# A fused kernel's first batch: the engines' order up to the first gate product written by hand, one normaliser chain, and a tile for every raw weight

## The chip, the cores and the metric

The kernel runs on one core of a Trainium2 chip. The core has TensorE (PE) for matrix products, VectorE (DVE), ScalarE (ACT) and GpSimd (POOL) for work on elements, and DMA queues; the ones used here are issued from SyncE (SP) and from ScalarE. The metric is the device time of one execution in microseconds (us), as the median of several runs.

## What is computed

Three layers follow each other, for batches of 576 rows:

```python
kv  = einsum('bhsd,bhde', k, v)                       # linear attention, 8 heads of 64
out = einsum('bhsd,bhde->bhse', q, kv)
x   = out / sqrt(mean(out**2, -1) + 1e-6) * g_norm    # the normaliser
xk, xr = (mu * x + (1 - mu) * x_prev for mu in (mu_k, mu_r))   # x_prev: the row before
x2  = sigmoid(xr @ w_r) * (maximum(xk @ w_k, 0)**2 @ w_v)      # gate, keys, values
# then four experts of causal attention on x2, two per row by a gate
```

The inputs are float32, the weights w_r, w_k, w_v float64.

## The kernel before

There are eight batches of 576 x 512. Phase a does the linear attention, the gate and the keys, phase v the values, phase 2 the experts. The change is in phase a alone.

**Products.** Every float32 operand of a large product is split into a high and a low word (`split`), and a product is three of those (`mm3`): high by high, high by low, low by high. One group is 128 columns of weight by half a batch (288 rows), 12 products; a batch has 8 gate groups (`r_group`) and 16 key groups (`k_group`). They share four PSUM accumulators named `acc`.

**Weights.** w_r (4 pieces) and w_k (8 pieces of 128 x 512) come as 64-bit words, into tiles named `raw` or, for four of them, into the space of batch 1's `xT`; so at most four pieces can be under way. `converted` makes the two words of a piece: Abs on ScalarE, five steps on VectorE, copies on ScalarE, and three products with the identity on TensorE that correct the low word (L225 to L227). w_v is converted later, in `value_blocks`, which also builds the sums that phase v needs.

**The front of a batch** (`front`): k by v in five chunks (L293), the state copied to `kv` (L297), the queries by the state in four groups into `po` (L314), each evacuated by a Square and a copy (L318, L319), the means of the squares on TensorE (L332), the normaliser `rsqrt` on VectorE (14 steps, L338 to L353, result `rb`), spread back by TensorE (L361), and the scaling of `xT` (L364). For batch 0 this is done in two halves of 288 rows, each with its own chain. `mix` then makes the operands `mixh` and `mixl` from x and the row before: one ScalarE product (L416), one VectorE sum (L417), a copy (L418) and a subtraction (L410). For the gate of batch 0 the subtraction is done by TensorE and ScalarE instead (L406 to L408).

**Order.** The program is written as interleaved generators: `wconv` takes the next piece of weight, `wstep` one step of it between steps of the normaliser. What is written is not the final order. A scheduler simulates the program and orders each engine's instructions by its own times and priorities, and so draws forward what is ready. SP's queue loads k, v and q, then the small vectors; ScalarE issues the raw weights.

Of the kernel before, what the change touches and what calls it, by code (L numbers as in the profile page):

```python
# [25 lines left out]
def tile_kernel(ctx: ExitStack, tc: tile.TileContext, qT, k, v, g2, mu_k, mu_r, w_r, w_k, w_v, w_qk, w_vg, w_o, out):  # L26
# [31 lines left out]

    def split(hi, lo, src):
        nc.scalar.activation(hi, src, AF.Copy)  # L60
        nc.vector.tensor_sub(lo, src, hi.bitcast(F32))  # L61

    def mm3(ps, wh, wl, xh, xl, n):
        for i in range(n):
            nc.tensor.matmul(ps, wh(i), xh(i), start=(i == 0), stop=False)  # L65
            nc.tensor.matmul(ps, wh(i), xl(i), start=False, stop=False)  # L66
            nc.tensor.matmul(ps, wl(i), xh(i), start=False, stop=(i == n - 1))  # L67
# [102 lines left out]
    def phase_a():  # L170
        W["vb"] = ExitStack()
        vb = W["vb"].enter_context(tc.tile_pool(name="vb", bufs=1, side="right", reuse_waits="tile"))
        for name in BLOCKS:
            blk[name] = [vb.tile([P, KH, HM], F32R, name=f"w{u}_{name}") for u in "hl"]
        with ExitStack():
# [15 lines left out]
            first = []  # L191
            for b in range(2):
                first.append(sb.tile([P, NP, S + 1], F32, name="xT", bufs=2))
            spare = first[1].rearrange("p k t -> p (k t)")
            stg_ = ExitStack()
            stg = stg_.enter_context(tc.tile_pool(name="stg", bufs=1, side="right", reuse_waits="tile"))

            def low_word(lo, hi, ti, out, scale):
                nc.vector.tensor_scalar(hi, ti, -0x800000, None, op0=ALU.bitwise_and)
                yield  # L200
                nc.vector.scalar_tensor_tensor(out, lo.bitcast(U32), scale, hi.bitcast(F32), op0=ALU.mult, op1=ALU.mult)
                yield

            def high_word(hi, t):
                ti = t.bitcast(I32)
                nc.scalar.activation(t, hi.bitcast(F32), AF.Abs)
                yield
                nc.vector.tensor_scalar(t, t, TINY64, None, op0=ALU.max)
                yield
                nc.vector.tensor_scalar(ti, ti, 3, 0x3FFFFFF8, op0=ALU.logical_shift_left, op1=ALU.bitwise_and)  # L210
                yield
                nc.vector.scalar_tensor_tensor(ti, hi, -0x40000000, ti, op0=ALU.bitwise_and, op1=ALU.bitwise_or)
                yield
# [4 lines left out]
            def converted(raw, t, h, l):  # L218

                lo, hi = raw[:, :, 0], raw[:, :, 1]  # L220
                yield from high_word(hi, t)
                nc.scalar.activation(h, t, AF.Copy)
                yield from low_word(lo, hi, t.bitcast(I32), l, -2.0 ** -52)
                acc = acc_tile()
                nc.tensor.matmul(acc, ident, t, start=True, stop=False)  # L225
                nc.tensor.matmul(acc, idn, h, start=False, stop=False)
                nc.tensor.matmul(acc, idn, l, start=False, stop=True)  # L227
                nc.scalar.activation(l, acc, AF.Copy)

            wts = []  # L230
            raws = {}

            def wload(i):
                if i < len(wts):
                    _, _, w, r0, c0 = wts[i]
                    if i in (2, 3, 6, 7):
                        flat = spare[:, i % 2 * 2 * CW:(i % 2 + 1) * 2 * CW].bitcast(I32)
                    else:
                        flat = stg.tile([P, 2 * CW], I32, name="raw", bufs=2)
                    raws[i] = flat.rearrange("p (n t) -> p n t", t=2)  # L240
                    nc.scalar.dma_start(flat, w[r0:r0 + P, c0:c0 + CW].bitcast(I32))

            wat, cur = [0], []

            def wstep():
                if cur:
                    next(cur[0], None)

            def wconv():
                i = wat[0]  # L250
                wat[0] += 1
                if cur:
                    for _ in cur.pop():
                        pass
                if i < len(wts):
                    h, l, *_ = wts[i]
                    cur.append(converted(raws[i], fr.tile([P, CW], F32, name="cvt", bufs=3), h, l))
                    wstep()
                if 0 < i < 7 or 8 < i < 11:
                    wload(i + (3 if i < 7 else 1))  # L260
# [3 lines left out]
            def load_kv(i):  # L264
                b, c = divmod(i, NF)
                if b < B and i not in kvt:
                    t0, n = FH[c]
                    kt, vt = [fr.tile([P, DM], F32, name=name, bufs=5) for name in ("kt", "vt")]
                    nc.sync.dma_start(kt[:n], k[b, t0:t0 + n, :])
                    nc.sync.dma_start(vt[:n], v[b, t0:t0 + n, :])  # L270
                    kvt[i] = (kt, vt)

            def load_q(i):
                b, c = divmod(i, 4)
                if b < B and i not in qts:
                    qt = fr.tile([P, 2, HS], F32, name="qt", bufs=4)
                    nc.sync.dma_start(qt, qT[b, c])
# [4 lines left out]
            def front(b):  # L282
                kvp = acc_tile()
                kv = fr.tile([P, NP, D], F32, name="kv", bufs=1)
                kw = kvp[:, :NP * D].rearrange("p (a e) -> p a e", a=NP)
                for c, (t0, n) in enumerate(FH):
                    kt, vt = kvt[b * NF + c]
                    for a in range(NP):

                        for r in range(2):  # L290
                            hd = 2 * (2 * (a // 2) + r) + a % 2
                            hd = slice(hd * D, (hd + 1) * D)
                            nc.tensor.matmul(kw[r * D:(r + 1) * D, a, :], kt[:n, hd], vt[:n, hd],  # L293
                                             start=(c == 0 and a == 0), stop=(c == NF - 1), skip_group_check=True)
                    if b > 0 or c < 3:
                        load_kv((b + 1) * NF + c)
                nc.scalar.activation(kv, kw, AF.Copy)  # L297
                yield
                yield
                xT = xTs[b] = first[b] if b < 2 else sb.tile([P, NP, S + 1], F32, name="xT", bufs=2)  # L300
                nc.gpsimd.memset(xT[:, :, 0:1], 0.0)
                sqs = {}

                def cols(h):
                    return slice(1 + h * HS, 1 + (h + 1) * HS)

                def heads(h, a):
                    i = 4 * b + 2 * h + a
                    qt = qts[i]
                    po = pf.tile([P, 2, 512], F32, name="po", bufs=2)  # L310
                    for c in range(2):
                        for r in range(2):
                            rs = slice(r * D, (r + 1) * D)
                            nc.tensor.matmul(po[c * D:(c + 1) * D, r, :HS], kv[rs, 2 * a + c, :], qt[rs, c, :], start=True, stop=True, skip_group_check=True)  # L314
                    if b > 0:
                        load_q(i + 4)
                    sq = sqs[h, a] = fr.tile([P, 2, HS], F32, name="sq", bufs=4)
                    nc.scalar.activation(sq, po[:, :, :HS], AF.Square)  # L318
                    nc.scalar.activation(xT[:, 2 * a:2 * a + 2, cols(h)], po[:, :, :HS], AF.Copy)  # L319

                sm = []
                QS = HS // 2
                ms, y, nt, rb = [fr.tile([P, QS], F32 if name != "rb" else F32R, name=name) for name in ("ms", "y", "nt", "rb")]

                def means(*hs):
                    if not sm:
                        sm.append(acc_tile())
                    for i in range(NP):
                        for h in hs:
                            for c in range(2):  # L330
                                g = 32 * (2 * h + c)
                                nc.tensor.matmul(sm[0][g:g + 32, :QS], sels[:, i, :], sqs[h, i // 2][:, i % 2, c * QS:(c + 1) * QS],  # L332
                                                 start=(i == 0), stop=(i == NP - 1), skip_group_check=True)

                def rsqrt(h0, h1):
                    g = slice(64 * h0, 64 * h1)
                    m, r, t, c = ms[g], y[g], nt[g], rb[g]
                    nc.vector.tensor_scalar(m, sm[0][g, :QS], -0.5, -0.5e-6, op0=ALU.mult, op1=ALU.add)  # L338
                    wstep()
                    nc.vector.tensor_scalar(t.bitcast(I32), m.bitcast(I32), 1, None, op0=ALU.logical_shift_right)  # L340
                    wstep()
                    nc.vector.tensor_scalar(r.bitcast(I32), t.bitcast(I32), -1.0, float(0x5F3759DF + 2 ** 30 - 2 ** 22), op0=ALU.mult, op1=ALU.add)
                    wstep()
                    for _ in range(3):
                        nc.vector.tensor_mul(t, r, r)
                        wstep()
                        nc.vector.tensor_mul(t, t, m)
                        wstep()
                        nc.vector.scalar_tensor_tensor(r, t, 1.5, r, op0=ALU.add, op1=ALU.mult)
                        wstep()  # L350

                    nc.vector.tensor_copy(c, r)
# [726 lines left out]
```

## Time and profile before

| | us |
|---|---|
| median of 3 runs (lowest, highest) | 1014.84 (1014.62, 1015.19) |
| the profiled execution, its span | 1015.07, 1013.2 |
| busy: TensorE, VectorE, ScalarE, GpSimd | 966.5, 638.1, 540.6, 417.1 |

TensorE is busy 95% of the span. The page's 40 slices, about 25 us each, show that its idle time is nearly all in the first six and that its clock is below full there. A profile's busy TensorE isn't the same as TensorE at full speed: it may run at a lower granted clock.

### The profile page before, as it was taken

Reading aid. Unit: us, or ns where it says so; the run is one execution under the profiler, and the core shown is the slowest. Engines: PE = TensorE matmul, PEld = TensorE weight load, DVE = VectorE, ACT = ScalarE, POOL = GpSimd, SP = SyncE. Lnnn points to the kernel's source line nnn. Section 1 sums busy time; section 2 is a strip of 40 time slices with the busy share of each in tenths; the row PEclk is TensorE's granted clock in tenths of the full one; section 3 lists DMA queues with packets and bytes.
Section 4 is the critical chain, followed back from the end, with each engine's and each line's share of the span. In section 5 each row is a group of like instructions: output and inputs, shape, how many; then the busy total and the mean of one; then the engine's idle time right before and its main releaser. Section 6 shows DMA issues by size and latency. Waiting matters only on the chain.

```text
span 1013.2 us, 21245 instructions
## 1 busy us (share of the span) xinstructions
PE 966.5 (95%) x7960; PEld 877.9 (87%) x7960; DVE 638.1 (63%) x1538; ACT 540.6 (53%) x1334; POOL 417.1 (41%) x510
## 2 busy tenths in 40 slices
PE   5679989999999999999999999999999999999998
PEld 2359879998999999999899999888989888888986
DVE  4868978455463726359888885566575555656552
ACT  4666666555565655545444443356463645464544
POOL 0005545131222213276787777445161625334321
PEclk8889989999999999999999999999999999999999
DMA  9563362635446322676676652202020202020102
GB/s 349 160 197 124 120 222 91 209 107 185 159 134 191 105 80 77 197 251 200 212 241 202 209 165 94 71 22 60 37 79 17 94 2 95 22 73 27 48 13 82
DMA packets 82742, 127.22 MB, mean 126 GB/s; under 512 B 7632, under 2 KB 58320, under 8 KB 82640
## 3 DMA queue, kind: packets, MB, share of 16 engines
q1 hardware_dynamic: 63152, 97.68, 29.3%
q10 hardware_dynamic: 19488, 28.19, 8.7%
q8 instruction: 63, 1.03, 0.4%
q14 instruction: 39, 0.32, 0.1%
HBM read 78.66 MB, written 47.19 MB: 124 GB/s over the span
## 4 chain that ended last, share of the span: by engine, by line
PE 73%; DVE 8%; DMA 8%; ACT 5%; POOL 4%; issue 2%; SPq 0%; ACTq 0%; DVEq 0%; POOLq 0%
PE acc L65 15%; PE acc L66 15%; PE acc L67 14%; PE qa L629 6%; PE qd L629 4%; PE acc L629 4%; PE pt L898 3%; PE acc L925 3%; DMA x2in<-x2d 3%; PE s L849 3%; POOL x2l L735 2%; ACT pr L861 2%; DMA vraw<-in_w_v 2%; PE po L314 1%; POOL pr L878 1%
## 5 line engine op out<-in xcount | busy, mean ns | idle before, releaser
L447 POOL TENSOR_TENSOR ksq<-rl 128x288 f32<-128x288 f32 x128 | 96.8, 760 | 168.8 <-ACT rl L445 132.0
L66 PE MATMUL acc<-mixl,wkh 128*128 128x288 f32 x512 | 153.4, 300 | 0.0
L65 PE MATMUL acc<-mixh,wkh 128*128 128x288 f32 x512 | 151.8, 296 | 0.0
L67 PE MATMUL acc<-mixh,wkl 128*128 128x288 f32 x512 | 150.7, 294 | 0.0
L878 POOL TENSOR_SCALAR pr<-pr,rc,wg 128x512 f32<-128x512 f32 (+3 forms) x128 | 76.7, 613 | 100.3 <-DVE wg L808 53.2
L861 ACT ACTIVATE pr<-pr,nm 128x256 f32<-128x256 f32 (+4 forms) x144 | 83.2, 579 | 65.0 <-DVE nm L815 64.8
L410 DVE TENSOR_TENSOR mixl<-xm,mixh 128x288 fp32r<-128x288 f32 x120 | 57.4, 514 | 91.3 <-ACT mixh L418 83.9
L66 PEld LDWEIGHTS acc<-mixl,wkh 128*128 128x128 f32 x512 | 96.4, 188 | 1.6
L641 POOL TENSOR_TENSOR sgv<-ct,sgv 128x288 f32<-128x288 f32 x64 | 82.4, 1313 | 35.2 <-DVE ct L639 34.7
L67 PEld LDWEIGHTS acc<-mixh,wkl 128*128 128x128 f32 x512 | 96.6, 189 | 0.0
L445 ACT ACTIVATE rl<-acc 128x288 f32<-128x288 f32 x128 | 51.8, 405 | 83.7 <-PE acc L67 66.5
L65 PEld LDWEIGHTS acc<-mixh,wkh 128*128 128x128 f32 x512 | 96.3, 188 | 0.1
L65 PE MATMUL acc<-mixh,wrh 128*128 128x288 f32 x256 | 78.9, 309 | 0.4 <-ACT rl L445 0.4
L815 DVE CUSTOM_DVE_ANT_0 pr<-s,mask 128x256 f32<-128x256 f32 (+4 forms) x144 | 66.9, 482 | 18.6 <-PE pt L898 11.8
L66 PE MATMUL acc<-mixl,wrh 128*128 128x288 f32 x256 | 76.7, 300 | 0.2 <-ACT mixl L408 0.2
L67 PE MATMUL acc<-mixh,wrl 128*128 128x288 f32 x256 | 76.5, 299 | 0.0
L65 PE MATMUL acc<-x2h,wqh 128*128 128x320 f32 (+1 forms) x240 | 74.3, 310 | 0.0
L67 PE MATMUL acc<-x2h,wql 128*128 128x320 f32 (+1 forms) x240 | 71.1, 296 | 0.0
L66 PE MATMUL acc<-x2l,wqh 128*128 128x320 f32 (+1 forms) x240 | 70.9, 295 | 0.0
L61 DVE TENSOR_TENSOR kk<-tv,kk 128x1152 fp32r<-128x1152 f32 x32 | 59.0, 1861 | 8.8 <-ACT kk L60 8.8
L898 PE MATMUL pt<-ident,pr 128*128 128x128 f32 x400 | 62.7, 276 | 1.1 <-ACT pt L907 0.5
L418 ACT ACTIVATE mixh<-xm 128x288 fp32r<-128x288 f32 x128 | 52.3, 443 | 10.2 <-DVE xm L417 10.1
(209 smaller groups left out, 2778.6 us busy)
## 6 DMA issues: line engine op xcount, KB each, us to landing
kkd<-ksq SPq DMA_DIRECT2D x128, 144.0 KB, 1.8
kin<-kkd SPq DMA_DIRECT2D x32, 576.0 KB, 4.9
qt<-in_qT SPq DMA_DIRECT2D x32, 288.0 KB, 4.6
sgd<-sg ACTq DMA_DIRECT2D x64, 144.0 KB, 2.8
sgv<-sgd SPq DMA_DIRECT2D x16, 576.0 KB, 3.8
x2d<-sgv SPq DMA_DIRECT2D x16, 576.0 KB, 2.8
out<-ob SPq DMA_DIRECT2D x28, 288.0 KB, 2.1
kt<-in_k SPq DMA_DIRECT2D x24, 256.0 KB, 4.5
```

The lines of the kernel that those rows point to most:

```text
L61: nc.vector.tensor_sub(lo, src, hi.bitcast(F32))
L65: nc.tensor.matmul(ps, wh(i), xh(i), start=(i == 0), stop=False)
L66: nc.tensor.matmul(ps, wh(i), xl(i), start=False, stop=False)
L67: nc.tensor.matmul(ps, wl(i), xh(i), start=False, stop=(i == n - 1))
L410: nc.vector.tensor_sub(xl[:, p, :], xp, xh[:, p, :].bitcast(F32))
L447: nc.gpsimd.tensor_mul(sq, rl, rl)
L629: nc.tensor.matmul(q[:, :HS], a[:, i, ms_], c[:, i, :], start=(start and i == 0 and n == 0), stop=(stop and i == KH - 1 and n == 2), skip_ ...
L641: nc.gpsimd.tensor_mul(g, c, g)
L815: nc.vector.tensor_tensor_reduce(out=pr[:R, k0:k0 + kn], in0=s[:R, :kn], in1=mk, scale=1.0, scalar=lo, op0=ALU.add, op1=ALU.min, accum_out ...
L861: nc.scalar.activation(pr[:, :L], pr[:, :L], AF.Exp, bias=nm, scale=-1.0, accum_out=sms[b, p, j][:, e2:e2 + 1])
L878: nc.gpsimd.tensor_scalar(pr[:, :L], pr[:, :L], rc[:, r:r + 1], wg, op0=ALU.mult, op1=ALU.mult)
L898: nc.tensor.transpose(pt[:, (i - i0) * P:(i - i0 + 1) * P], pr[:, k1 - P:k1], ident)
```

## The change

- While a flag is on, `vec`, `act` and `ten` (wrappers of the three engines) mark each instruction to be kept in program order. The flag is on from the first weight conversion to the fourth gate group of batch 0. The steps of pieces 5 and 6 of the weights, written behind that point, are not marked, and the scheduler may place them among the marked ones.
- Batch 0's front is written out: four w_r pieces with the chunks of k by v, all four query groups, one means, one normaliser chain over 128 rows, then per half the spreading, scaling and mixing, then four gate groups.
- All twelve raw pieces have tiles of their own, in the space that the w_v blocks use later. All but two are loaded by SP, the small vectors first.
- The low half of batch 0's gate operand is a subtraction on VectorE like everywhere else; `older` issues the ScalarE product of the next quarter a step earlier.
- Batch 0's keys do four column groups for both halves first, then the other four; w_k's second half is converted between them. Batch 0's gates are stored through SP.
- In `value_blocks` the Abs and the load of each w_v piece are kept in program order; the order of the sums changes, and work starts four groups later.

```diff
+    class InOrder:
+        def __getattr__(self, name):
+            f = getattr(self.engine, name)
+            return (lambda *a, **k: tc.keep_in_program_order(f(*a, **k))) if self.on else f
...
+            def wload(i, eng):
+                _, _, w, r0, c0 = wts[i]
+                raw = vb.tile([P, CW, 2], I32, name="raw", tag="blk", bufs=2 * len(BLOCKS))
+                eng.dma_start(raw.rearrange("p n t -> p (n t)"), w[r0:r0 + P, c0:c0 + CW].bitcast(I32))
...
                 def low(p):
-                    if b == 0 and which == "r":
-                        acc = acc_tile()
-                        nc.tensor.matmul(acc[:, :HS], ident, xp, start=True, stop=False)
-                        nc.tensor.matmul(acc[:, :HS], idn, xh[:, p, :], start=False, stop=True)
-                        nc.scalar.activation(xl[:, p, :], acc[:, :HS], AF.Copy)
...
+                    vec.tensor_sub(xl[:, p, :], xs[p], xh[:, p, :].bitcast(F32))
...
+            for u, src in ((g_sb, g2), (muk, mu_k), (mur, mu_r)):
+                nc.sync.dma_start(u, src)
+            for i in range(KD):
+                wload(i, (act, nc.sync)[i % 2])
...
+            for i in range(KD, len(wts)):
+                wload(i, nc.sync)
...
-            TK = [1, 0, 1, 1, 0, 1, 1, 1, 1, 1, 1]
-            wconv()
-            for i in range(7):
-                run(f0)
-                ticks(TK[i])
...
+            for e in (vec, act, ten):
+                e.on = True
...
+            for h in range(2):
+                for a in range(2):
+                    f0.heads(h, a)
+            run(cs[4])
+            f0.means()
+            f0.rsqrt()
+            run(cs[4])
...
+                for _ in mix(0, h, "r"):
+                    pass
+            f1.start()
             for m in range(KD):
                 r_group(0, 0, m)
+            for e in (vec, act, ten):
+                e.on = False
...
+            WK = [(8,), (8, 9, 8, 8), (8, 9), (9, 10, 9), (9, 10), (10, 11, 10), (10, 11), (11, 11, 11)]
...
-            for b in range(B):
+            for b in range(1, B):
```

The order that results, at three places. VectorE, kernel before, from the means of the first half (`ms`) into its chain; `nt` and `y` are the chain's, `cvt` and `raw` pieces of w_k:

```order
L338 TENSOR_SCALAR ms_268<-acc_317 64x144
L212 SCALAR_TENSOR_TENSOR cvt_365<-raw_265,cvt_365 128x512
L340 TENSOR_SCALAR nt_270<-ms_268 64x144
L208 TENSOR_SCALAR cvt_387<-cvt_387 128x512
L199 TENSOR_SCALAR raw_265<-cvt_365 128x512
L342 TENSOR_SCALAR y_269<-nt_270 64x144
L210 TENSOR_SCALAR cvt_387<-cvt_387 128x512
L201 SCALAR_TENSOR_TENSOR wkl_134<-raw_265 128x512
L345 TENSOR_TENSOR nt_270<-y_269 64x144
L212 SCALAR_TENSOR_TENSOR cvt_387<-raw_293,cvt_387 128x512
L347 TENSOR_TENSOR nt_270<-nt_270,ms_268 64x144
L199 TENSOR_SCALAR raw_293<-cvt_387 128x512
```

The same place in the changed kernel, where all rows marked L67 are kept in order:

```order
L67 TENSOR_SCALAR y_374<-nt_375 128x144
L213 TENSOR_SCALAR cvt_531<-cvt_531 128x512
L67 TENSOR_TENSOR nt_375<-y_374 128x144
L215 TENSOR_SCALAR cvt_531<-cvt_531 128x512
L213 TENSOR_SCALAR cvt_558<-cvt_558 128x512
L67 TENSOR_TENSOR nt_375<-nt_375,ms_373 128x144
L217 SCALAR_TENSOR_TENSOR cvt_531<-raw_160,cvt_531 128x512
L215 TENSOR_SCALAR cvt_558<-cvt_558 128x512
L67 SCALAR_TENSOR_TENSOR y_374<-nt_375,y_374 128x144
L204 TENSOR_SCALAR raw_160<-cvt_531 128x512
L217 SCALAR_TENSOR_TENSOR cvt_558<-raw_162,cvt_558 128x512
L67 TENSOR_TENSOR nt_375<-y_374 128x144
```

The chain now spans 128 rows and stands once; steps of w_k pieces (here two at a time) still stand between its steps, ten in all where the first chain had sixteen.

ScalarE, kernel before, from the first sigmoid (`sg`) on; `vraw` is a piece of w_v, `kv_558` batch 1's state:

```order
L436 ACT_TABLE_LOAD
L436 ACTIVATE sg_541<-acc_542 128x288
L437 DMA sgd0_73<-sg_541 128x288
L222 ACTIVATE wkh_133<-cvt_676 128x512
L458 DMA vraw_1368<-in_w_v 128x1024
L297 ACTIVATE kv_558<-acc_557 128x256
L228 ACTIVATE wkl_134<-acc_632 128x512
L436 ACTIVATE sg_641<-acc_642 128x288
L437 DMA sgd0_73<-sg_641 128x288
L206 ACTIVATE cvt_1444<-vraw_1368 128x512
L416 ACTIVATE xm_622<-xT_128,nur_89 128x288
```

ScalarE, changed kernel, from the second half's operand copies (`mixh_443`) to the sigmoids of the first half's gate groups:

```order
L67 ACTIVATE mixh_443<-xm_447 128x288
L67 ACTIVATE xm_456<-xT_307,nur_89 128x288
L67 ACTIVATE mixh_443<-xm_451 128x288
L394 ACTIVATE xm_671<-xT_307,nuk_88 128x288
L67 ACTIVATE mixh_443<-xm_456 128x288
L67 ACT_TABLE_LOAD
L67 ACTIVATE sg_467<-acc_468 128x288
L67 ACTIVATE sg_483<-acc_484 128x288
L394 ACTIVATE xm_673<-xT_307,nuk_88 128x288
L67 ACTIVATE sg_499<-acc_500 128x288
```

The loads and the Abs of w_v are gone from here, and the first sigmoid now stands behind the last operand copy of the second half.

SP's queue, kernel before, from its eleventh row; ten loads of k (`kt`) and v (`vt`) stand ahead, `qt` are queries:

```order
L277 DMA qt_160<-in_qT 128x576
L277 DMA qt_162<-in_qT 128x576
L277 DMA qt_165<-in_qT 128x576
L277 DMA qt_167<-in_qT 128x576
L513 DMA g_sb_85<-in_g2 128x1
L514 DMA muk_86<-in_mu_k 128x4
L515 DMA mur_87<-in_mu_r 128x4
L269 DMA kt_207<-in_k 128x512
```

SP's queue, changed kernel, from its first row:

```order
L504 DMA g_sb_85<-in_g2 128x1
L504 DMA muk_86<-in_mu_k 128x4
L504 DMA mur_87<-in_mu_r 128x4
L228 DMA raw_124<-in_w_r 128x1024
L228 DMA raw_128<-in_w_r 128x1024
L262 DMA kt_130<-in_k 128x512
L263 DMA vt_131<-in_v 128x512
L262 DMA kt_134<-in_k 128x512
```

The three small loads moved ahead of everything, and two w_r pieces ahead of k and v; the eight w_k pieces follow the queries.

## Rows read from the trace of the kernel before

**Rows 1.** busy time by stage: us, PE, PEld, DVE, ACT, POOL (x instructions), clock, DMA

```profile
0.00:52.30 52.30, 31.75 (x200) 17.20 (x201) 33.10 (x85) 27.71 (x52) 1.99 (x17) 0.87 0.73 247
52.30:88.20 35.90, 30.66 (x274) 23.56 (x273) 26.50 (x57) 25.38 (x58) 7.01 (x6) 0.90 0.59 182
88.20:116.05 27.85, 27.61 (x211) 26.81 (x210) 24.53 (x55) 15.09 (x40) 17.01 (x20) 1.00 0.34 114
116.05:173.45 57.40, 51.45 (x450) 46.26 (x449) 48.27 (x96) 37.50 (x93) 27.54 (x32) 0.94 0.47 157
173.45:408.30 234.85, 234.85 (x2242) 220.25 (x2241) 117.73 (x270) 133.96 (x325) 57.58 (x84) 1.00 0.42 137
```

**Rows 2.** whom TensorE waited for: us in total, times, longest

```profile
PE po L361 <- DVE rb L353: 5.6, 3, 4.8
```

**Rows 3.** TensorE in order of time: start, us, line, out<-in, count

```profile
52.33 0.30 PE L65 MATMUL acc<-mixh,wrh 128*128 128x288 f32 x1
...
57.18 1.13 PE L225 MATMUL acc<-cvt,ident 128*128 128x512 f32 x2
...
58.60 0.29 PE L65 MATMUL acc<-mixh,wrh 128*128 128x288 f32 x1
...
84.05 0.93 PE L332 MATMUL acc<-sq,sels 128*32 128x144 f32 x20
...
88.20 0.29 PE L65 MATMUL acc<-mixh,wkh 128*128 128x288 f32 x1
...
89.80 0.29 PE L65 MATMUL acc<-mixh,wkh 128*128 128x288 f32 x1
...
101.13 0.67 PE L361 MATMUL po<-rb,selb 32*128 32x144 f32 x8 [0.24 <-DVE rb L353]
...
117.97 2.55 PE L293 MATMUL acc<-vt,kt 128*64 128x64 f32 x80
...
127.27 1.20 PE L314 MATMUL po<-qt,kv 64*64 64x288 f32 x16 [2.71 <-ACT kv L297]
```

**Rows 4.** the start on TensorE, ScalarE and in the chain of waits

```profile
17.41 1.15 PE L293 MATMUL acc<-vt,kt 112*64 112x64 f32 x32
...
19.97 0.63 ACT L222 ACTIVATE wrh<-cvt 128x512 fp32r<-128x512 f32 x1 [2.79 <-DVE nuk L517]
...
22.87 0.65 ACT L318 ACTIVATE sq<-po 128x576 f32<-128x576 f32 x1 [1.36 <-PE po L314]
...
23.95 0.66 ACT L318 ACTIVATE sq<-po 128x576 f32<-128x576 f32 x1
...
14.35 5.36 DMA muk<-in_mu_k
```

**Rows 5.** the normaliser on VectorE, first half of batch 0, then batch 2

```profile
28.14 0.30 DVE L338 TENSOR_SCALAR ms<-acc 64x144 f32<-64x144 f32 x1 [1.52 <-PE acc L332]
...
38.00 0.35 DVE L353 SCALAR_TENSOR_TENSOR rb<-rb,lom,y 64x144 fp32r<-64x144 f32 x1
...
191.34 0.31 DVE L338 TENSOR_SCALAR ms<-acc 128x144 f32<-128x144 f32 x1 [1.50 <-PE acc L332]
...
196.05 0.37 DVE L353 SCALAR_TENSOR_TENSOR rb<-rb,lom,y 128x144 fp32r<-128x144 f32 x1
```

**Rows 6.** the first low-half operand copy on ScalarE

```profile
41.74 0.43 ACT L418 ACTIVATE mixh<-xm 128x288 fp32r<-128x288 f32 x1
```

**Rows 7.** four microseconds after a pause of TensorE, columns as in rows 1

```profile
142.00:146.00 4.00, 4.00 (x22) 3.59 (x16) 2.41 (x7) 2.19 (x6) 0.95 (x2) 0.50 0.66 205
```

**Rows 8.** the DMA queue of SP from 420 to 440 us: packets, MB, share

```profile
q1 hardware_dynamic: 3966, 5.64, 83.6%
```

**Rows 9.** a w_v piece on ScalarE, TensorE behind it, its landing

```profile
65.82 0.66 ACT L206 ACTIVATE cvt<-vraw 128x512 f32<-128x512 f32 x1 [5.02 <-DMA vraw<-in_w_v]
...
67.51 1.33 PE L406 MATMUL acc<-xm,ident 128*128 128x288 f32 x2 [3.52 <-DVE xm L417]
...
58.36 7.43 DMA vraw<-in_w_v
```

More of the change, by code (lines that the diff above doesn't have):

```diff
@@ L243, in phase_a @@
[L243 to L260, printed above, removed]
+            wts, raws = [], []
@@ L321, in front @@
[L321 to L327, printed above, removed]
+                            ten.matmul(po[c * D:(c + 1) * D, r, :HS], self.kv[rs, 2 * a + c, :], qt[rs, c, :], start=True, stop=True, skip_group_check=True)
+                    load_q(i + 4)
+                    sq = self.sq[h, a] = fr.tile([P, 2, HS], F32, name="sq", bufs=4)
@@ L381, in front, with cols @@
+            QS = HS // 2
+            def cols(h):
+                return slice(1 + h * HS, 1 + (h + 1) * HS)
+            def front(b):
+                f = Front(b)
+                f.start()
+                for c in range(NF):
+                    f.chunk(c)
+                f.state()
+                yield
+                yield
                 for h in range(2):
                     for a in range(2):
-                        heads(h, a)
+                        f.heads(h, a)
                     yield
@@ new lines, in phase_a @@
+            f0, f1 = Front(0), Front(1)
+            run(cs[0])
+            f0.start()
+            for i in range(KD):
+                run(cs[i])
+                if i + 1 < KD:
+                    run(cs[i + 1])
+                run(cs[i])
+                run(cs[i])
+                if i == KD - 1:
+                    f0.chunk(NF - 1)
+                    f0.state()
+                run(cs[i])
+                if i < KD - 1:
+                    f0.chunk(i)
+                if i == KD - 2:
+                    f0.chunk(i + 1)
@@ new lines, in phase_a @@
+            mk = mix(0, 0, "k")
+            for m in range(KD + 1):
+                run(mk)
+                if m < 3:
+                    f1.chunk(m + 2)
+            f1.state()
+            mk = mix(0, 1, "k")
+            WK = [(8,), (8, 9, 8, 8), (8, 9), (9, 10, 9), (9, 10), (10, 11, 10), (10, 11), (11, 11, 11)]
+            mr = chain(mix(1, 0, "r"), mix(1, 1, "r"))
+            for n, (m0, h, m) in enumerate([(m0, h, m) for m0 in (0, KD) for h in range(2) for m in range(KD)]):
+                k_group(0, h, m0 + m)
+                if n < 4:
+                    f1.heads(*halves[n])
+                    run(mk)
+                if n == 3:
+                    run(mk)
+                for i in WK[n] if n < len(WK) else ():
+                    run(cs[i])
+                if n == 7:
+                    f1.means()
+                    f1.rsqrt()
+                if 8 <= n < 10:
+                    for a in range(2):
+                        f1.scaled(n - 8, a, f1.spread(n - 8, a))
+                if n > 10:
+                    run(mr, mr)
@@ L608, in phase_a @@
                         pass
-                    cvp[0].close()
             stk.close()
```

366 lines of the change are left out of this document (172 added, 194 removed).

## The prediction

> **What bounds the kernel now.** I read the table of busy time by stage first. I cut it at TensorE's first products of each stage: the first gate product at 52.3 us, the first key product of batch 0 at 88.2, the first product of batch 1 at 116.05, of batch 2 at 173.45, of batch 7 near 408. From 173.45 on TensorE is busy without a break at full clock: 234.85 us for five batches, 46.97 each [rows 1]. Nothing can be won there by order alone. Before that it is idle for 52.3 - 31.75 = 20.55, then 5.24, 0.24 and 5.95 us, 32.0 in all, and the granted clock is 0.87, 0.90 and 0.94 of full in three of the four stages. Batch 1 takes 57.40 where a later one takes 46.97, so 10.4 us are lost there alone. The table of waits then tells who is late: the largest single wait, 4.8 us, is for the normaliser `rb` [rows 2]. So the start and batches 0 and 1 are the whole question. On every engine the order after the w_v conversion, phases v and 2 included, is the same row for row, so what is won by 173 us should last to the end.
>
> **The change, part by part.** The work that TensorE must do is priced at full clock. One weight conversion (three products) goes from 57.18 to 58.60, 1.42 us; one group of twelve products from 88.20 to 89.80, 1.60; a batch's 80 k-by-v products 2.55; half of its query products 1.20; 20 of 32 passes of the means 0.93, so 1.5 a batch; half of the spreading 0.67, so 1.3 a batch [rows 3].
>
> *Start to the normaliser.* In the kernel before, the last k-by-v products ended at 17.41 + 1.15 = 18.56 us. The copy of the state came later, because on ScalarE it stood behind a weight copy that waited 2.79 us, by the profile for `nuk`, that is for the small load of mu_k that landed at 14.35 + 5.36 = 19.71 [rows 4]. The small loads now go first, so this wait goes. The added wait is that VectorE's first conversion steps now stand behind `nuk` and `nur`, and behind them ScalarE's copies and TensorE's checks of the first weight. The slowest landing seen, 5.36 us, would put them at about 7 us; this is inside the next bounds. The query products can begin no earlier than the w_r, k and v of batch 0 land (2.1 + 2.4 MB; 5.64 MB took 83.6% of 20 us on SP's queue alone, 337 GB/s while busy [rows 8], so 13.2 us after a start at about 2 us: 15), and on the rows of before no later than about 19. Three products of the last w_r piece now stand ahead of them. I take 18.0. Putting almost all loads on SP's queue I cost at nothing by the same row.
>
> All four query groups run now before the means, where two did before. Each costs ScalarE a Square and a copy, 23.95 - 22.87 = 1.08 us [rows 4]: 18.0 + 0.6 for the first products + 4.3, and the means end at about 23.0.
>
> *The normaliser.* One chain of 128 rows replaces two of 64. In the order its 14 steps have ten w_k conversion steps among them, since those are not pinned. Before, the first chain ran from 28.14 to 38.35, with 16 conversion steps: 30 steps in 10.2 us, 0.34 each. The bare chain of a later batch took 191.34 to 196.42, 5.1 us [rows 5]. These are the two ends; 24 steps at 0.34 give 8.2, and `rb` at 31.2.
>
> *To the first gate product.* Before, 38.35 to the first operand copy's end at 42.17 are 3.8 us [rows 6]. Four conversion steps now stand between, some 1.2 us beyond what lay there before. The first gate product comes at 31.2 + 5.0 = 36.2, against 52.33. The first group can't end before the fourth low half, about 3.3 us later: 39.5.
>
> *The gate stage.* From 39.5 TensorE has seven more groups (11.2), four conversions (5.7) and 2.55 of k by v: 19.4. Two waits come on top. TensorE restarts after a pause, and after such a pause it ran for four microseconds at 0.50 of its clock, 1.2 GHz [rows 7]; that costs 2.0. And the first sigmoid now stands on ScalarE behind the last operand copy of the second half (the second piece of the order), while one of the four accumulators is held for batch 1's state: the fourth group must wait for it, about 2.3. So the key products begin at 39.5 + 19.4 + 4.3 = 63.2 (before: 88.2, with batch 1's queries already done).
>
> The Trainium skill, "TensorE: Matmul & The Clock Gate", Part 1, says that the penalty of the clock's ramp is under 1% of a typical span and need not be fitted. By that the 2.0 would be dropped and the result would be 988. The rows put 0.50 into just these stretches, so I keep it.
>
> *The key stage of batch 0* now holds 16 groups (25.6), two halves of the queries (2.4), four conversions (5.7), the means and the spreading (2.8): 36.5, and batch 1 begins at 99.7 instead of 116.05: 16.4 us earlier. The second half of w_k is asked for only after eight groups, 13 us on; that hides its conversion.
>
> *Batch 1.* Before, its stage was crowded by all eight w_v pieces, which the scheduler had drawn forward, the first to 58 us [rows 9]. Now their Abs and their loads are pinned and lie in batches 1 to 6. I take the later batches' 46.97 plus 0.5 for a tight hand-over of the second half's operands: 9.9 gained. For the w_v steps spread over six dense batches I add 1.0; VectorE is busy there 117.73 of 234.85 us [rows 1], which is the cover.
>
> *Dropped and added steps.* The 16 low-half products of batch 0 and their eight copies on ScalarE go; eight subtractions on VectorE come, and they are inside the 3.3 above. The operand's older term is issued one step earlier in every mix; in the dense batches this is worth nothing.
>
> *Sum.* The profiled execution took 1015.07 (span 1013.2 and 1.9 around it), 0.2 above the median of 1014.84. 1015.07 - 16.4 - 9.9 + 1.0 = 989.8; I say 990.
>
> **Rivals.** *A: the w_v work hurts where it is put.* Its eight pieces with their adds on GpSimd now fall on batches that have no slack on TensorE. If each piece costs TensorE one 1.0 to 1.3 us stall, 8 to 10 us go: 998. For it speaks that the same pieces had a crowded batch 1 before; against it the half idle VectorE. The Trainium skill, "SBUF — State Buffer", Terms, says that VectorE and GpSimd lock a shared port pair against each other for a whole instruction; no row here separates that, and it would make this rival likelier.
>
> *B: ScalarE bounds the gate stage.* Between the first sigmoid and batch 1's state copy stand 35 of its instructions against 14.7 us of products on TensorE. At the 0.54 of a Square's slot (half of 1.08) they are 18.9, 4.2 more; with one more fall of the clock, 4 us, the result is 998.
>
> *C, the other side: a pinned Abs waits for its w_v piece.* Before, ScalarE once stood 5.02 us at such an Abs and TensorE 3.52 behind it, with a load that took 7.43 to land [rows 9]. With 2 us for the clock after such a pause, eight times 5.5 are 44: 1034, slower. In the order at least six groups, 9.6 us, lie between load and Abs, so it decides only where landings exceed that, and five of the eight must.
>
> *D: the change doesn't do what it says.* The pin orders only the pinned instructions, and the w_k steps among the chain grow to before's 16 and more, with late pieces to wait for; the gate products would start at about 45 and the result be 1000.
>
> *E: better.* The chain takes 5.1 to 6 and the accumulator wait is hidden: 984.
>
> **How the numbers follow.** The forecast, 984 to 996, 0.62; E below that 0.06; A 0.14; B 0.09; D 0.05; C 0.04. The range is 981 to 1003, which leaves out C, the far ends of A and B, and the best of E. Within 0.2% (2 us) is about what a measurement here can't tell from no change. All cases but C lie well below 1013: faster 0.93, same 0.02, slower 0.05, the last with a little for a start that goes wrong in a way not named.
>
> **What would show it.** The first gate product at 34 to 39 us; `rb` some 8 us after the means; a wait of TensorE before the fourth gate group; the first product of batch 1 at 97 to 103, and of batch 2 some 47.5 later. If batches 2 to 6 take over 47.5 each, A is right; idle TensorE between 45 and 63 with ScalarE full is B; an Abs of `vraw` that waits for its DMA is C. The forecast is wrong if batch 1 starts after 106, or if the gain by batch 2 is not still there at the end.

## The result, and the profile after

The changed kernel takes 998.30 us (median of 4 runs, 996.78 to 1002.44); the kernel before, run beside it, 1015.02 (4 runs, 1014.62 to 1016.80). The ratio is 0.9838, 95% interval 0.9806 to 0.9870. The gain is clear of the noise. The time lies inside the stated range of 981 to 1003, but outside the 984 to 996 of the forecast itself and 8 us above its 990. The profiled execution took 996.78, its span 995.0.

The busy table of the kernel after, TensorE alone (us, busy, instructions, clock, DMA share, GB/s), is cut at the first products of the same stages as [rows 1]: first gate product, first key product, batches 1 to 7.

```profile
0.00:38.05 38.05, 17.50 (x177) 0.88 0.97 333
38.05:62.62 24.57, 23.77 (x192) 0.90 0.30 102
62.62:100.18 37.56, 37.56 (x290) 1.00 0.44 136
100.18:150.35 50.17, 48.72 (x450) 1.00 0.51 161
150.35:201.16 50.81, 48.94 (x450) 0.97 0.50 160
201.16:248.45 47.29, 47.02 (x450) 1.00 0.50 167
248.45:295.42 46.97, 46.97 (x450) 1.00 0.52 169
295.42:342.60 47.18, 47.03 (x450) 1.00 0.52 166
342.60:389.93 47.33, 47.33 (x450) 1.00 0.23 79
389.93:995.00 605.07, 590.26 (x4594) 1.00 0.32 105
```

Batch 1 begins at 100.18 in place of 116.05, and batch 1 takes 50.17 in place of 57.40. But batches 2 to 6 take 239.58 together where before they took 234.85 [rows 1], and what follows lasts as long as before (605.07 against 1013.2 - 408.32 = 604.88). So 15.87 + 7.23 were won and 4.73 + 0.19 given back: 18.2, the difference of the spans.

The start, on VectorE and then TensorE (start, us, engine, line, out<-in, and in brackets the idle time before and who ended it; L67 is the helper through which all hand-ordered instructions pass):

```profile
25.13 0.31 DVE L67 TENSOR_SCALAR ms<-acc 128x144 f32<-128x144 f32 x1 [6.73 <-PE acc L67]
...
28.95 0.68 DVE L217 SCALAR_TENSOR_TENSOR cvt<-raw,cvt 128x512 int32<-128x512 int32 x1
...
33.16 0.37 DVE L67 SCALAR_TENSOR_TENSOR rb<-rb,lom,y 128x144 fp32r<-128x144 f32 x1
```

```profile
33.67 1.13 PE L67 MATMUL po<-rb,selb 32*128 32x144 f32 x8 [8.59 <-DVE rb L67]
...
38.05 0.61 PE L67 MATMUL acc<-mixh,wrh 128*128 128x288 f32 x1
...
47.78 0.40 PE L77 MATMUL acc<-mixh,wrh 128*128 128x288 f32 x1 [0.49 <-ACT sg L67]
```

`rb` is ready 8.4 us after the chain's first step (before: two chains, 28.14 to 38.35 for the first alone [rows 5]). The steps at L213 to L217 among them are w_k's. TensorE's wait for `rb`, 8.59 us, is the largest of the kernel after its first instruction, but it comes at 33.7 now.

Batch 1's loss. VectorE in the normaliser of batch 2's rows:

```profile
119.74 0.31 DVE L329 TENSOR_SCALAR ms<-acc 128x144 f32<-128x144 f32 x1 [0.83 <-PE acc L323]
121.77 0.43 DVE L213 TENSOR_SCALAR cvt<-cvt 128x512 f32<-128x512 f32 x1 [1.72 <-ACT cvt L211]
...
124.71 0.30 DVE L335 SCALAR_TENSOR_TENSOR y<-nt,y 128x144 f32<-128x144 f32 x1
125.05 1.35 DVE L333 TENSOR_TENSOR nt<-y 128x144 f32<-128x144 f32 x1
126.43 0.66 DVE L334 TENSOR_TENSOR nt<-nt,ms 128x144 f32<-128x144 f32 x1
...
130.92 0.37 DVE L338 SCALAR_TENSOR_TENSOR rb<-rb,lom,y 128x144 fp32r<-128x144 f32 x1
```

The chain takes 11.5 us where the bare one took 5.1 [rows 5]. A w_v piece stands between its steps, and the second instruction in the queue waits 1.72 us for that piece's Abs on ScalarE, with the chain behind it. Then steps that take 0.30 take 0.66 to 1.35. TensorE waits 1.45 us for this `rb`. The Abs itself comes late (121.08): ten microseconds before, ScalarE stood in front of the store of a gate tile, until a load of k had landed.

```profile
110.72 0.41 ACT L420 ACTIVATE sg<-acc 128x288 f32<-128x288 f32 x1 [2.16 <-DMA kt<-in_k]
```

Batch 2's loss. ScalarE (ACTq rows are DMAs that it issues), then TensorE:

```profile
156.81 0.34 ACTq L446 DMA_DIRECT2D vraw<-in_w_v  x1
...
162.79 0.33 ACTq L421 DMA_DIRECT2D sgd<-sg  x1
163.16 0.65 ACT L314 ACTIVATE sq<-po 128x576 f32<-128x576 f32 x1 [4.42 <-DMA vraw<-in_w_v]
```

```profile
164.41 0.71 PE L311 MATMUL po<-qt,kv 64*64 64x288 f32 x8 [1.87 <-ACT xT L315]
```

ScalarE stands for 4.42 us in front of the *store* of a gate tile, until the load of the next w_v piece has landed (issued at 156.81, landed 5.9 us later); the evacuation of the query products is queued behind it. TensorE stands 1.87 us, and this pause costs once more: from 166 to 169 the granted clock is 0.50, and its mean over 166 to 170 is 0.61.

```profile
162.00:166.00 4.00, 2.13 (x23) 0.96 1.06 312
166.00:170.00 4.00, 4.00 (x25) 0.61 0.91 287
170.00:174.00 4.00, 4.00 (x54) 1.00 0.26 86
```

Why should a store wait for a load? In the list of ScalarE's instructions both, in rows 193 and 197, name the same completion counter (a number that a DMA raises when it has landed):

```
193 L446 DMA vraw<-in_w_v 128x1024 [waits DMAHW6_49]
195 L421 DMA sgd_75<-sg 128x288 [waits DMAHW2_49,Activation_49]
197 L421 DMA sgd_75<-sg 128x288 [waits DMAHW6_49,Activation_49]
198 L314 ACTIVATE sq<-po 128x576 [waits PE_49]
```

The DMAs of SyncE and ScalarE take turns on eight counters, and a DMA waits until the one before it on its counter is done. The store of batch 1 shares its counter with the k load in the same way. That is theory 1; the rival is that the DMA engines are simply full there (share 1.06).

### The profile page after: what moved, and what is told of

The parts are those of the page before. It is cut to its first block, busy times and chain, and to the rows that moved or that the text cites. A ratio compares the mean times of both kernels' runs of the same rounds, so it can differ in the third digit from the quotient of the medians.

```text
span 995.0 us, 21152 instructions
## 1 busy us (share of the span) xinstructions
PE 955.1 (96%) x7936; PEld 871.4 (88%) x7936; DVE 643.1 (65%) x1532; ACT 538.8 (54%) x1326; POOL 414.4 (42%) x510
## 3 DMA queue, kind: packets, MB, share of 16 engines
q8 instruction: 63, 1.03, 0.4%
## 4 chain that ended last, share of the span: by engine, by line
PE 74%; DVE 8%; DMA 6%; ACT 6%; POOL 3%; issue 2%; SPq 0%; ACTq 0%; DVEq 0%; POOLq 0%
PE acc L77 15%; PE acc L78 14%; PE acc L79 14%; PE qa L671 6%; PE qd L671 4%; PE acc L671 4%; PE pt L940 3%; PE acc L967 3%; DMA x2in<-x2d 3%; PE s L891 3%; ACT pr L903 2%; POOL x2l L777 2%; PE acc L294 2%; POOL pr L920 1%; DMA vt<-in_v 1%
## 5 line engine op out<-in xcount | busy, mean ns | idle before, releaser
L397 DVE TENSOR_TENSOR mixl<-xm,mixh 128x288 fp32r<-128x288 f32 x120 | 59.8, 530 | 50.1 <-ACT mixh L403 49.6
L77 PE MATMUL acc<-mixh,wrh 128*128 128x288 f32 x240 | 73.9, 308 | 0.5 <-ACT sg L67 0.5
L79 PE MATMUL acc<-mixh,wrl 128*128 128x288 f32 x240 | 72.1, 300 | 0.0
L78 PE MATMUL acc<-mixl,wrh 128*128 128x288 f32 x240 | 72.0, 300 | 0.0
L72 ACT ACTIVATE kk<-tv 128x1152 fp32r<-128x1152 f32 x32 | 37.3, 1167 | 38.5 <-POOL tv L160 15.6
```

Source lines behind the costliest of these rows:

```text
L77: ten.matmul(ps, wh(i), xh(i), start=(i == 0), stop=False)
L78: ten.matmul(ps, wh(i), xl(i), start=False, stop=False)
L79: ten.matmul(ps, wl(i), xh(i), start=False, stop=(i == n - 1))
L397: vec.tensor_sub(xl[:, p, :], xs[p], xh[:, p, :].bitcast(F32))
```

## The experiments

All comparisons are with runs of the kernel before on the same chip. The table gives, from each profiled run, the start of the first gate product, of the first key product, of batches 1, 2, 3 and 7, the time from batch 7 to the end, and the median and ratio of the timed runs.

| kernel | gate | key | b1 | b2 | b3 | b7 | rest | median | ratio, interval |
|---|---|---|---|---|---|---|---|---|---|
| before | 52.33 | 88.20 | 116.05 | 173.45 | 220.43 | 408.32 | 604.9 | 1015 to 1017 | 1 |
| after | 38.05 | 62.62 | 100.18 | 150.35 | 201.16 | 389.93 | 605.1 | 998.30 | 0.9838 (0.9806-0.9870) |
| e2_store_sp | 38.12 | 62.69 | 100.24 | 148.78 | 196.11 | 384.32 | 607.8 | 994.22 | 0.9781 (0.9766-0.9795) |
| e1_load_sp | 39.17 | 63.73 | 101.28 | 153.14 | 201.72 | 395.57 | 605.7 | 997.35 | 0.9820 (0.9786-0.9854) |
| e3_later | 38.51 | 63.07 | 100.63 | 149.19 | 196.15 | 392.09 | 605.0 | 999.86 | 0.9825 (0.9787-0.9864) |
| e4_unpinned | 39.31 | 63.87 | 104.52 | 159.75 | 214.38 | 402.27 | 606.3 | 1010.19 | 0.9936 (0.9919-0.9952) |
| e5_pin_only | 52.34 | 84.08 | 111.60 | 160.47 | 208.50 | 404.35 | 605.2 | 1011.31 | 0.9956 (0.9932-0.9980) |
| e6_free_order | 38.03 | 62.39 | 99.95 | 150.24 | 204.24 | 393.67 | 610.2 | 1005.83 | 0.9885 (0.9864-0.9906) |
| e7_two_chains | 42.52 | 67.65 | 105.22 | 157.37 | 210.53 | 399.61 | 609.9 | 1011.04 | 0.9935 (0.9910-0.9960) |
| e8_best | 38.49 | 63.05 | 100.61 | 149.16 | 196.13 | 384.35 | 605.0 | 992.18 | 0.9758 (0.9735-0.9780) |
| e9_chain_clear | 34.15 | 59.50 | 97.48 | 146.03 | 193.01 | 381.22 | 609.1 | 992.11 | 0.9757 (0.9734-0.9780) |
| e11_kv_first | 44.02 | 69.18 | 106.73 | 155.28 | 202.26 | 390.47 | 608.0 | 1000.07 | 0.9837 (0.9815-0.9859) |
| e12_kv_clear | 40.68 | 64.13 | 102.42 | 150.97 | 197.95 | 386.70 | 607.3 | 994.61 | 0.9780 (0.9756-0.9804) |
| e13_tail_kept | 33.69 | 60.45 | 97.53 | 146.09 | 193.06 | 381.46 | 608.2 | 990.72 | 0.9741 (0.9723-0.9759) |

### Who holds ScalarE up in batch 2

**e2_store_sp**

```diff
-(nc.sync if b == 0 else act).dma_start(sgd[b][:, m, h * HS:(h + 1) * HS], sg)
+nc.sync.dma_start(sgd[b][:, m, h * HS:(h + 1) * HS], sg)
```

> Of the changed kernel, all stores of the gate (sgd) are issued by SyncE; ScalarE issues only the w_v loads. Theory 1: in batch 2 ScalarE stood 4.42 us because its store waits for the completion counter that the w_v load just issued also uses; with the stores on SyncE ScalarE has no such wait, batch 2 takes 47.0 to 48.0 us in place of 50.81, batch 1 keeps its slow normaliser chain (49.0 to 50.2), the whole is 993 to 996 us. Theory 2: the DMA engines, full at that time (share 1.0), are what delays, whoever issues: SyncE then holds its k and v loads back behind the stores, TensorE waits for kt or qt in their place, batch 2 stays at 50 to 51 and the whole at 997 to 1000.

```profile
100.24:148.78 48.54, 48.54 (x451) 1.00 0.53 166
148.78:196.11 47.33, 47.33 (x450) 1.00 0.54 171
156.00:162.00 6.00, 6.00 (x57) 1.00 1.03 330
```

Batches 1 and 2 lose their waits, with the DMA engines as busy as before (0.54, 171 GB/s). Where the stall had been, their share is 1.03 and the w_v load takes 7.7 us to land, yet TensorE is busy throughout. Theory 1 holds: full DMA engines go with a late landing, but alone they don't stop TensorE.

Batch 1 was expected to keep its slow chain (49.0 to 50.2) and takes 48.54:

```profile
119.94 0.30 DVE L329 TENSOR_SCALAR ms<-acc 128x144 f32<-128x144 f32 x1
...
128.59 0.77 DVE L338 SCALAR_TENSOR_TENSOR rb<-rb,lom,y 128x144 fp32r<-128x144 f32 x1
```

The w_v piece still stands among the steps and the chain still takes 9.4 us, but ScalarE no longer stands in front of a store in batch 1, the Abs comes at 118.86 in place of 121.08, and TensorE reaches `rb` at 129.75 without a wait. So the losses of both batches go with the stores.

One thing was not expected: the rest after batch 7 takes 2.7 us more. Of these, 1.6 are TensorE's own busy time: behind a wait of 1.77 us its clock is 0.63 from 456.3 to 460.3.

**e1_load_sp** (`act.dma_start` of the w_v load becomes `nc.sync.dma_start`)

> Of the changed kernel, the w_v loads are issued by SyncE, the stores of the gate stay on ScalarE. Theory 1 (shared counter): the w_v load falls on another counter in the list of waits; the stores of batch 2 then wait for k and v loads at most (landing 4.0 to 7.4 us after issue, issued earlier), ScalarE stands 0 to 2.5 us, batch 2 takes 47 to 49, the whole 994 to 997. Theory 2 (full DMA engines): the same bytes move in the same 10 us, ScalarE stands 3 us or more in front of a store, batch 2 50 to 51, the whole 997 to 1000.

The wait for `vraw` is gone from ScalarE. In its place stand waits of stores for k and v loads that precede them on their counters, in batches 1, 2, 4 and 5:

```profile
ACT sg L420 <- DMA vt<-in_v: 3.8, 2, 2.6
ACT sq L314 <- DMA kt<-in_k: 3.6, 1, 3.6
```

Batch 2 is 48.58 as expected, though ScalarE stands 3.6 us in it and not 2.5 at most; batch 1 is 51.86, batch 5 50.33. Moving the load only changes who is waited for, and the median, 997.35, lies between the two theories. (The profiled run is the slowest of its four, 1003.14; the others are 994.99 to 997.82.)

**e3_later** (`range(6)` becomes `range(14)` in `value_blocks`: the first w_v step comes eight groups later)

> Of the changed kernel, the first step of the w_v conversion comes 14 groups into batch 1 in place of 6, behind the normaliser chain of batch 2's rows. Theory A: the 11.5 us of that chain (119.7 to 131.3) come from the steps of the w_v piece that stand between its steps on VectorE; they are gone, the chain takes 5 to 6 us, TensorE's 1.45 us before the first spread are gone, batch 1 takes 48.0 to 49.0. Batch 2 has its w_v load elsewhere; it loses 0 to 4 us by whether a store shares its counter. The whole 993 to 998. Theory B: the chain is slow because of what GpSimd and ScalarE do there anyway (squares of the keys, Relu); it stays over 9 us and batch 1 over 49.8.

```profile
120.11 0.31 DVE L329 TENSOR_SCALAR ms<-acc 128x144 f32<-128x144 f32 x1 [0.87 <-PE acc L323]
...
124.08 0.70 DVE L337 CAST rb<-y 128x144 fp32r<-128x144 f32 x1
124.81 0.37 DVE L338 SCALAR_TENSOR_TENSOR rb<-rb,lom,y 128x144 fp32r<-128x144 f32 x1
```

Theory A holds for the chain: with the w_v piece elsewhere it takes 5.07 us in place of 11.5, TensorE no longer waits for it, and batch 1 takes 48.56. But no store holds ScalarE up in batch 1 here either, and e2 took TensorE's wait away with the piece left in the chain; so what the piece alone cost TensorE isn't shown. Batch 2 is clean too, 46.96; but now batch 4 takes 49.31 and batch 5 52.71, the latter by the same kind of wait, and the whole, 999.86, misses the 993 to 998 expected:

```profile
299.00 0.34 ACTq L446 DMA_DIRECT2D vraw<-in_w_v  x1
...
305.29 0.33 ACTq L421 DMA_DIRECT2D sgd<-sg  x1
305.66 0.65 ACT L314 ACTIVATE sq<-po 128x576 f32<-128x576 f32 x1 [4.71 <-DMA vraw<-in_w_v]
```

Here load and store share counter DMAHW4. The stall has moved with the turn of the counters.

### What the parts of the change are worth

**e4_unpinned** (`pinned = tc.keep_in_program_order` becomes `pinned = lambda i: i`) and **e5_pin_only** (the kernel before, with w_v's loads and Abs held in program order)

> Of the changed kernel, the w_v loads and the Abs that opens each piece are not held in program order. Theory A: the pin bought part of batch 1's 7.2 us; without it the scheduler puts the pieces of w_v early again, two or three of them beside the front of batch 2, batch 1 takes 53 to 57 us, later batches 47, the whole 1000 to 1005. Theory B: batch 1 gained because the conversions of w_k are elsewhere and buffers are free, not by the pin; batch 1 stays at 49.5 to 51, the whole within 2 us of 998.

> The kernel before, with one part of the change alone: its w_v loads and the Abs that opens each w_v piece are held in program order. Theory A: the pin is what takes the crowd out of batch 1 (without it, batch 1 of the changed kernel took 55.23 us and batch 2 54.63, with it 50.17 and 50.81); here batch 1 falls from 57.40 to 48 to 52, later batches stay within 3 us of 46.97 in sum, the whole 1007 to 1012. Theory B: in the kernel before, the w_v steps are hemmed in by the conversion of w_k and by the shared staging buffers, the pin alone moves nothing or makes a piece wait: batch 1 stays over 55, the whole 1013 to 1020.

In e4 batch 1 takes 55.23, batch 2 54.63: theory A, and its whole, 1010, is still above the 1000 to 1005 expected, since batch 0 also grew (65.21 against 62.13). In e5 batch 1 falls from 57.40 to 48.87, theory A again, and the gate stage from 35.87 to 31.74. But batches 2 to 6 give back 243.88 - 234.85 = 9.0 us, where 3 were allowed; ScalarE waits there for k, v and w_v loads, up to 4.8 us at once.

Against the kernel before, the pin alone gains 5.7 us, the rest of the change alone 6.2, both together 16.7. That is 4.8 more than their sum; whether each needs the other isn't shown, since waits elsewhere moved totals by as much in other runs (e6).

**e6_free_order** (`e.on = True` is never set)

> Of the changed kernel, nothing is held in program order up to the first gate group (the loads, tiles, one normaliser chain and the pins of w_v stay). Theory A: the order written by hand is what brings the first gate product from 52.33 to 38.05; without it the scheduler puts the conversion of w_k between the steps of the chain, and the first gate product comes at 42 to 50, the whole 1002 to 1010. Theory B: the loads in another order and the one chain do it; the first gate product comes at 37 to 40, the whole 996 to 1000.

Theory A is false as to the place. With the order left to the scheduler the first gate product comes at 38.03, as with the order written by hand (38.05); the chain begins 4.2 us later but has one w_k step between its own. Batch 1 begins at 99.95. The 7.5 us that it is slower come behind: batch 2 takes 54.00, 3.2 more, batch 5 48.11, the rest 610.2, 5.1 more.

```profile
ACT sq L314 <- DMA vraw<-in_w_v: 6.1, 1, 6.1
```

That is the store behind the w_v load once more, in batch 2. In the rest the scheduler's order is another one, and TensorE waits 3.7 us for an operand `vs` that cost it no wait before. So the hand-written order by itself bought nothing that this start shows, and a total can move by 7 us through places far from the edit.

**e7_two_chains**

```diff
-            f0.rsqrt()
+            f0.rsqrt(0, 1)
+            f0.rsqrt(1, 2)
```

> Of the changed kernel, batch 0's normaliser runs as two chains of 64 partitions, one behind the other, as in the kernel before (batch 1 on: one chain). Theory A: a step takes as long for 64 partitions as for 128, so 11 more steps of 0.31 to 0.36 us stand in front of the first scaled rows: the first gate product comes 3.5 to 5 us later, at 41.5 to 43, and as the gate stage runs back to back the whole is 3 to 5 us more. Theory B: steps on half the partitions are shorter or the first half's spread hides them; under 1.5 us more.

```profile
33.58 0.31 DVE L67 TENSOR_SCALAR ms<-acc 64x144 f32<-64x144 f32 x1
...
37.78 0.37 DVE L67 SCALAR_TENSOR_TENSOR rb<-rb,lom,y 64x144 fp32r<-64x144 f32 x1
```

A step takes 0.30 us on 64 partitions as on 128; the second chain adds 4.57 us, the first gate product comes 4.47 later, batch 1 5.04 later. That is theory A. The whole loses 12.7, more than the 3 to 5 expected: batches 1 and 2 take 52.15 and 53.16, the rest 609.9. The trace places most of it: ScalarE stands in front of the same two stores as in the changed kernel, now for 2.60 and 5.56 us, TensorE waits 1.46 and 2.96 behind them, and the clock of the two batches is 0.97 and 0.94; in the rest TensorE waits 3.8 for `vs`, as in e6. Why these waits are longer is open. Of the 14.28 us that the first gate product gained, the single chain is thus about 4.5; the remaining 9.8 are left to the loads and tiles by subtraction, not by a run of their own.

### Putting it together

**e8_best** (stores on SyncE except in the last batch, `range(14)`)

> Of the changed kernel, stores of the gate go to SyncE except in the last batch, and the first w_v step comes 14 groups into batch 1. Both theories by the runs so far: the stores keep ScalarE free of waits for loads (batch 2 47.0 to 47.4), the later start keeps the w_v steps out of batch 1's chain (48.5), the last batch's stores on ScalarE give back the 2.7 us that the tail lost with all stores on SyncE. Theory A, the three add up: batch 7 begins at 382.5 to 384.5, the whole 988.5 to 992. Theory B, they don't: a w_v piece falls into another batch's chain or the tail loses from another cause: 993 to 996.

```profile
100.61:149.16 48.55, 48.55 (x450) 1.00 0.51 164
149.16:196.13 46.97, 46.97 (x450) 1.00 0.52 169
...
384.35:989.30 604.95, 590.02 (x4594) 1.00 0.32 105
```

Theory A: batch 7 begins at 384.35 and the rest takes 604.95, which fits e2's loss there having come with the last batch's stores. That isn't shown: e9 to e13 leave these stores on ScalarE, and their rest takes 607 to 609. The median, 992.18, is 0.2 above the range and beats both kernels.

**e9_chain_clear** (e8, with the Abs of the w_k pieces pinned behind the first gate operands)

> The kernel of e8_best, with the conversion of w_k held behind the first rows of the gate mix, so that none of its steps stands in batch 0's normaliser chain. Theory A: the 8.57 us from the means to rb are 5.07 of the chain and 3.5 of w_k steps between; they go, and 0.9 of w_k steps between rb and the first gate product too: the first gate product comes at 33 to 35 in place of 38.5, the gate stage takes 24.6 to 26, the whole gains 2.5 to 5 us on e8_best. Theory B: VectorE is busy 20.2 of 24.5 us in the gate stage already and the 8 us of w_k steps come back there: the gate stage grows by 3 to 5 us and the whole stays within 1.5 us of e8_best.

```profile
25.84 0.31 DVE L67 TENSOR_SCALAR ms<-acc 128x144 f32<-128x144 f32 x1 [6.93 <-PE acc L67]
...
30.09 0.37 DVE L67 SCALAR_TENSOR_TENSOR rb<-rb,lom,y 128x144 fp32r<-128x144 f32 x1
```

The chain is bare, 4.62 us, and the first gate product comes at 34.15, 4.34 earlier than in e8: theory A. The gate stage and the key stage take 0.8 and 0.4 longer, and batch 7 begins 3.13 earlier. The whole gains nothing, because the rest takes 609.1. Behind batch 7 the scheduler's order differs from e8's, and TensorE waits 3.3 us (two waits) for an operand `qs`, against 0.7 in e8; then its clock is 0.57 from 621.2 to 625.2, which costs 1.7.

**e11_kv_first, e12_kv_clear** (k, v and q of batch 0 loaded ahead of w_r, the query heads written among the conversions; e12 also with e9's edit)

> The kernel of e8_best, with batch 0's k and v loaded ahead of w_r and its products, query heads and means written ahead of the conversions they do not need. Theory A: the start is set by when k and v have landed (state at 18.25 behind 2 MB of w_r); with them first the state comes at 10 to 12, the means end at 18 to 20, and the conversion of w_r fills VectorE's empty 7 us there; the first gate product comes at 31 to 35 in place of 38.5, the whole gains 3 to 6 us. Theory B: w_r then lands last and its fourth piece ends the wait; the first gate product comes at 36 to 40, the whole within 2 us of e8_best.

> Both of the two edits, e9_chain_clear's and e11_kv_first's, on the kernel of e8_best. Theory A: the first gate product comes at 28 to 32, and what of it is kept is what VectorE's work up to the key stage allows; the whole gains 4 to 8 us on e8_best (984 to 988). Theory B: VectorE's work, 62 us of the first 100, fills the gate stage and gives it back; the key stage begins less than 3 us earlier than in e8_best (63.05), the whole 989 to 993.

Both miss both theories. In e11 the state does come at 12, but w_r lands last, and in the order that I wrote its products stand in front of the later query heads:

```profile
12.62 2.29 PE L67 MATMUL po<-qt,kv 64*64 64x288 f32 x16 [0.47 <-ACT kv L67]
...
36.18 2.07 PE L67 MATMUL acc<-cvt,ident 128*128 128x512 f32 x2 [8.12 <-DVE cvt L67]
```

The first gate product comes at 44.0, 5.5 later than in e8, not earlier; in e12 it comes at 40.68. An order by hand can be worse than the one it replaces.

**e13_tail_kept** (e9, the Abs of two w_k pieces one group earlier)

> The kernel of e9_chain_clear, with the Abs of two w_k pieces one gate group earlier. Behind batch 7 the scheduler then writes VectorE's and ScalarE's order as in e8_best, which e9_chain_clear's differed from (an accumulator eviction of the last attention's queries stands one step later there, and TensorE waits 2.8 us for it). Theory A: e9_chain_clear had won 3.13 us up to batch 7 and lost 4.1 behind it by that other order; here batch 7 begins at 380.5 to 382.5 and what follows takes 604.5 to 605.5 as in e8_best, the profiled span is 985 to 988, the whole 987 to 990. Theory B: the stretch behind batch 7 differs by what the DMA and the clock do in a run, not by the order; it takes 607 to 609, and the whole is 990 to 993.

By the numbers theory B: the order behind batch 7 on VectorE and ScalarE is e8's again, and the rest still takes 608.2. On TensorE one score product (`s`) stands twelve products later than in e8, as it does in e11; in e12, where TensorE's order is e8's, the rest takes 607.3.

```profile
622.65 0.39 PE L77 MATMUL acc<-wgh,x2h 128*128 128x260 f32 x1 [1.78 <-DVE ks L73]
```

```profile
621.46:625.46 4.00, 2.81 (x18) 0.81 0.01 2
625.46:629.46 4.00, 4.00 (x28) 0.76 0.00 0
```

TensorE waits 1.78 us here where it waits 1.40 in e8, and then its clock is 0.81 and 0.76, where e8's is 1.00 in the same stretch: 1.7 of the 3.3 us that the rest lost on e8. The other 1.5 are idle time. What causes them, and whether the product's place made the longer wait, is open. The median, 990.72, is the lowest of all, but its interval (0.9723 to 0.9759) overlaps e8's (0.9735 to 0.9780).

## Why the prediction was near, and where it was off

- *Start to the first gate product* (predicted 36.2): 38.05. The state came at 18.25 (predicted 18.0), the means ended 2.1 later than the 23.0 said, since the first query products waited for the last w_r check (19.66). The term "24 steps at 0.34", 8.2 us, measured 8.4, and e9 shows that the ten w_k steps in it are real: without them it is 4.62.
- *Gate stage* (key products at 63.2): 62.62. The clock term of 2.0 was 2.4 (clock 0.90 over 24.57 us). The 2.3 us for the fourth group's accumulator didn't occur; one wait of 0.49 stands a group later. The Trainium skill, "TensorE: Matmul & The Clock Gate", Part 1, calls the ramp under 1% of a span; 2.4 of 995 us is within that, yet it is not nothing, and batch 2's second ramp came on top.
- *Batch 1 begins* at 99.7: 100.18. Up to here the sum was off by 0.5, in part by luck: the start missed by +1.9, the gate stage (24.57 for 27.0) by -2.4, the key stage (37.56 for 36.5) by +1.1.
- *Batch 1*, "46.97 plus 0.5", failed: 50.17. Of the 2.7 us missing, e2 and e3 each give back 1.6 without the 1.45 us wait for the normaliser, and e2 does so with the w_v piece still in the chain. The other 1.1 or so stay in every variant that pins w_v on the new start (48.5): there TensorE's 80 k-by-v products of batch 2's rows come in four pieces, not in one; that was seen, not tested.
- *"For the w_v steps spread over six dense batches I add 1.0"* is the step that failed most: 4.73 measured, 3.8 of it in batch 2. VectorE's idle half was the cover I named, and VectorE was not the engine: ScalarE stood still, for a counter. 0.5 + 2.7 + 3.7 is the 7 us between 989.8 and the profiled 996.78.
- *Rival A* named the right amount (998) and the right place (the dense batches), but as a stall per piece; it was two stalls, not eight, so the amount came by luck. Its sign, over 47.5 in batches 2 to 6 each, holds for batch 2 alone; the others took 46.97 to 47.33. *Rival C* named ScalarE waiting for a w_v load with TensorE behind, but at the pinned Abs; no Abs waited, a store did. The prediction read each DMA's issue as free and did not look at the waits of the stores. *Rival D* did not occur: ten w_k steps stood in the chain, as in the order, and the gate products came at 38.05, not 45. (e4 tests the pins of w_v alone; without the others, in e6, the place is the same.) *Rival B* did not occur: TensorE waits under 1 us in the gate stage.
- The slow steps in batch 1's chain: the step of 1.35 us at 125.05 ends 0.2 us after an add on GpSimd that ran from 124.94 for 1.29, and in e3 the copy to `rb` (0.23 elsewhere) takes 0.70 beside a square on GpSimd at 124.02 of 0.67. By the Trainium skill, "SBUF — State Buffer", Terms (a port pair that one of the two holds for a whole instruction), this would be a lock; the traces agree in these places. The five chain steps from 125.05 to 129.25 took 4.06 us where five take 1.55: some 2.5 us of the 11.5.

## What to carry to other kernels

Before a DMA is moved or added, list for each store on a compute engine's queue which earlier DMA shares its completion counter: a store can hold up an engine for a load that has nothing to do with it, and stores belong on an engine that has nothing else to do. Work that is spread into "idle" slots is best kept off the short serial chains that everybody waits for: one later start shortened the chain by 6.5 us here, though what TensorE got back, 1.6 us, came by moving the stores as well. Price a change by stages, since a shift of one DMA moved stalls of 2 to 6 us from one batch to another and can hide what an edit is worth.

## What was not expected of the hardware

A pause of TensorE of 1.87 us in a run at full clock was followed by 0.61 mean clock over 166 to 170 us: 1.6 us more, nearly the price of the pause itself. The same came behind waits of 1.77 us in e2 and 1.78 in e13. And the changed kernel's four runs span 5.7 us, e2's four runs, without load-dependent stores on ScalarE, 1.2. That late transfers make this difference fits, but isn't shown: one run of each was traced.
